# FNet mixing with a gated conv FFN on one core: batch 0's feature row D/2 made by a small FFT at the start, and ScalarE in five weight narrowings

## The chip, the cores and the metric

The kernel runs on one core of one Trainium2 chip. The metric is the device time of one execution in microseconds (us). Before the change three executions took 1222.69, 1222.80 and 1223.03 us, median 1222.8. The profiled execution, from which all durations below come, has a span of 1222.2 us at a granted TensorE clock of 0.999.

## The reference

`x` has 8 batches of 3136 rows (sequence) and 256 columns (features), in fp32. The weights come in as 64-bit floats.

```python
X = np.fft.fft(np.fft.fft(x, axis=1), axis=2).real      # FNet mixing
h = np.maximum(X @ w_in, 0.0)                           # 256 -> 1024
conv_out[:, s] = sum_k conv_w[k] * h[:, s + k - 1]      # 3 taps, zero padded
out = (h * sigmoid(conv_out)) @ w_out                   # 1024 -> 256
```

## The kernel before, in words

**The mixing.** The sequence transform is cut by symmetry. `load_ops` (line 111) loads a batch in two halves: plain rows by SP, mirrored rows by POOL's indirect DMAs. `fold_ops` (line 143) adds and subtracts them on VectorE (DVE) into eight operands `w`. `units` (line 272) multiplies these by cosine and sine tables on TensorE (PE) and makes `PQ`, the transforms P and Q for half the frequencies. The other half follows by symmetry in each step. Half of the tables are loaded, the others are made from them by ScalarE (ACT) in `mirror_tables` (line 235), and `mend_row` (line 229) halves one row.

**The feature D/2.** One of the 129 independent feature columns, number 128, does not fit beside the others. For batches 1 to 7 class `Feature` (line 374) makes it by an FFT of 56 x 56: `gather` (line 417) reads 3136 single elements of `x` into `y`; `tables` (line 421) makes small twiddle tables on ACT; `stage` 0 and 2 (line 441) are small matmuls, 1 a multiplication on DVE, 3 a copy and a store to the DRAM row `ed`. `spread` (line 463) broadcasts the row to 128 partitions, `eb`. For batch 0 the row is made along the main path: `feature()` (line 327) with 16 one-column matmuls, its copies (line 345) and additions on POOL (lines 353 and 354), `row` and `flip` (lines 360 and 364), a store (line 369) and `spread`.

**The weights.** `narrow` (line 508) turns 64-bit floats into fp32 by seven DVE operations, lines 515 to 522: exponent bits out, bias changed, exponent shifted into place, sign put in, mantissa in two operations, product. `w_in` has four parts, `w_out` is narrowed in four of two chunks each. `blocks(i)` (line 587) multiplies the feature transform into part i of `w_in` and gives `G`; `column(i)` (line 604) does so for the feature D/2 and gives `ge`.

**The steps.** Work runs in 256 steps (batch, chunk of four, feature block of eight). In step s: `seed` (line 633) writes `eb * ge` into the PSUM tile `pa` on ACT; `products` (line 653) adds P in `pa` and puts Q in `pb`; in the first 20 steps, named triple, a third product adds Q to `pa` too. `copies` (line 664) moves to SBUF on ACT, `combine` (line 677) on DVE ends the row `h`, `first_tap` (ACT) and `other_taps` (DVE, line 694) are the convolution, `sigmoid` (ACT) and `gate` (DVE and POOL) follow, `mm2` (line 723) is the last product on PE. In the first four steps (`FIRST`) there is no seed: a 1-row product of `er` and `left` stands in its place (line 660), and steps 4 and 5 have a product by zeros (line 640).

**The order.** The schedule is by hand: each engine gets its instructions in the order of the code, and runs them in that order. The main loop is

```python
sigmoid(t-2); products(t+1); copies(t+1); run("act"); combine(t); run("dve")
seed(t+2); first_tap(t); other_taps(t-1); gate(t-2); run("load"); mm2(t-3); run("pe")
```

and a table `side` puts further work into a step: the narrowing of the last part of `w_in` into step 0, of `w_out` into steps 2, 3, 5 and 7, the folds of batch 1 into steps 9 to 19, `Feature` from step 5. Ahead of the loop come the loads, fold and units of batch 0. Two memsets of one element (lines 119 and 575) hold SP's second load and its table loads until POOL has issued its indirect loads. `keep_on` (line 748) issues 16 filler matmuls, in the order of PE ahead of the first unit. DMAs take one of eight semaphore lanes in turn, and a DMA waits until the one before on its lane has landed.

Of the kernel before, what the change touches and what calls it, by code (L numbers as in the profile page):

```python
# [30 lines left out]
FIRST = 4  # L31
# [7 lines left out]
def kernel(  # L39
# [33 lines left out]
    ep = ctx.enter_context(tc.tile_pool(name="ep", bufs=2))  # L73
    erp = ctx.enter_context(tc.tile_pool(name="erp", bufs=1))
# [28 lines left out]
    xh, wt, ea = {}, {}, {}  # L103
# [3 lines left out]
    sg = const.tile([P, 2, 2], F32, name="sg")  # L107
    nc.gpsimd.memset(sg[:, 0], -1.0)
    nc.gpsimd.memset(sg[:, 1], 1.0)
# [33 lines left out]
    def fold_ops(b):  # L143
# [3 lines left out]

        def half(h):
# [27 lines left out]
            def feats(odd):  # L176
                def f():
                    if h == 0 and odd:
                        wt[b] = [wp.tile([P, 4, HQ, P], F32, name="w", tag="w%d" % i) for i in range(2)]
                        if b == 0:  # L180
                            ea[b] = ep.tile([P, 2, HQ], F32, name="ea", tag="ea")
                            nc.gpsimd.memset(wt[b][0][0:KR, 2:4, :, P - 1:P], 0.0)
                    w, s = wt[b][odd], 6 * odd
                    v = t()[k, s:s + 2]
                    lo, hi = v[:, :, :, 1:P], v[:, :, :, D - 1:P:-1]
                    vt(w[k, 0:2, qs, 1:P], lo, hi, op=ALU.add)  # L186
                    vt(w[k, 2:4, qs, 0:P - 1], lo, hi, op=ALU.subtract)  # L187
                    nc.gpsimd.tensor_copy(w[k, 0:2, qs, 0], v[:, :, :, 0])
                    if b:
                        nc.gpsimd.memset(wt[b][odd][k, 2:4, qs, P - 1:P], 0.0)  # L190
                    elif odd:
                        gt(w[k, 2:4, qs, P - 1], t()[k, 7:5:-1, :, P], sg[k], op=ALU.mult)
                    else:
                        nc.gpsimd.tensor_copy(ea[b][k, :, qs], v[:, :, :, P])
                return f
# [9 lines left out]
    PQ, eb, er = {}, {}, {}  # L205
# [36 lines left out]
    class Unit:  # L242

        def __init__(self, b, mms, copy, fin, own=False):
            self.own, self.b, self.mms, self.copy_, self.fin_ = own, b, mms, copy, fin

        def matmuls(self, i, n):
            if i == 0:
                self.p = spare() if self.b == 0 and not self.own else psd.tile([P, 512], F32, name="pd", tag="pd")
            c = [len(self.mms) * j // n for j in (i, i + 1)]  # L250
            for f in self.mms[c[0]:c[1]]:
                f(self.p)
# [19 lines left out]
    def units(b):  # L272
# [54 lines left out]
        def feature():  # L327

            mms = []
            for i in range(2):  # L330
                for j, qs in enumerate(((3, 1), (2, 0))):
                    for c in range(2):
                        n = HO // 2 + 1 - c
                        o = 32 * (2 * j + c)
                        mms.append(product((slice(o, o + 1), slice(0, n)),
                                           lambda k, q, c=c: ea[b][0:k, c, q:q + 1], 0, qs[i],
                                           slice(c, HE, 2), i == 0, i == 1))

            def copy(p):
                a_["e"] = [asp.tile([P, HO + 2], F32, name="as", tag="as") for _ in range(2)]  # L340
                for j in range(2):
                    for c in range(2):
                        n = HO // 2 + 1 - c
                        o = 32 * (2 * j + c)
                        nc.scalar.copy(out=a_["e"][c][0:1, j * n:(j + 1) * n], in_=p[o:o + 1, 0:n])

            def fin(p):
                t = er[b]
                nh = HO // 2
                for c in range(2):  # L350
                    n = nh + 1 - c
                    a, bb = a_["e"][c][0:1, 0:n], a_["e"][c][0:1, n:2 * n]
                    gt(t[:, 2 * c:Q4 + 1:4], a, bb, op=ALU.add)
                    gt(t[:, M - 2 * c:Q4:-4], a[:, 0:nh], bb[:, 0:nh], op=ALU.subtract)
            return Unit(b, mms, copy, fin, True)

# [3 lines left out]
        def row():  # L360
            er[b] = erp.tile([1, NK], F32, name="er", tag="er")
            nc.sync.dma_start(out=er[b], in_=PQ[b][1][P - 1:P, :])

        def flip():

            act(er[b][:, 3:NK:4], er[b][:, 3:NK:4], AF.Copy, scale=-1.0)

        def store():
            nc.sync.dma_start(out=ed[b:b + 1, 0:NK], in_=er[b])

        return (begin, [odd_even(1), odd(1), even(1, 0), even(1, 1), feature(), odd_even(0), odd(0),
                        even(0, 0), even(0, 1)], row, flip, store)

    class Feature:

# [4 lines left out]
        def place(self):  # L380
            H, t = self.H, erp.tile([P, NK], F32, name="ft", tag="er")
# [24 lines left out]
            n = (RC + NQ - 1) // NQ  # L406
            self.l = [f[:, 0:2 * HE].rearrange("p (s i) -> p s i", s=2),
                      f[:, 2 * HE:2 * HE + 2 * H].rearrange("p (s i) -> p s i", s=2)]
            for r, v in enumerate(self.l):
                for s in range(2):  # L410
                    nc.gpsimd.memset(v[0:1, s], 1.0 - s)
                    w = v.shape[2]
                    nc.scalar.dma_start(out=v[1:1 + n * NQ, s], in_=bass.AP(
                        tensor=dft_seq.tensor, offset=dft_seq.offset + (2 * r + s) * NQ * HE,
                        ap=[[4 * NQ * HE, n], [HE, NQ], [1, w]]))

        def gather(self, b, b0):
            nc.sync.dma_start(out=self.y[self.K, b - b0].unsqueeze(2), in_=bass.AP(
# [44 lines left out]
    def spread(b, cs):  # L463

        for c in cs:
            ch = chunks[c]
            eb[b, c] = ebp.tile([P, HN], F32, name="eb", tag="eb")[:, 0:ch.k1 - ch.k0]
            nc.sync.dma_start(out=eb[b, c], in_=ed[b:b + 1, ch.k0:ch.k1].to_broadcast([P, ch.k1 - ch.k0]))
# [39 lines left out]
    def narrow(dst, raw):  # L508
# [7 lines left out]
        ts(out=d, in0=d, scalar1=-896, scalar2=0, op0=ALU.add, op1=ALU.max)  # L516
        ts(out=d, in0=d, scalar1=23, scalar2=None, op0=lsl)
        stt(out=d, in0=hi, scalar=-0x80000000, in1=d, op0=ALU.bitwise_and, op1=ALU.bitwise_or)

        ts(out=hi, in0=hi, scalar1=0xFFFFF, scalar2=0x100000, op0=ALU.bitwise_and, op1=ALU.bitwise_or)  # L520
        stt(out=lof, in0=lo.bitcast(U32), scalar=2.0 ** -32, in1=hi, op0=ALU.mult, op1=ALU.add)
        stt(out=dst, in0=lof, scalar=2.0 ** -20, in1=dst, op0=ALU.mult, op1=ALU.mult)

    class Weight:
# [14 lines left out]
        def narrow(self, c0, c1):  # L539
            if self.raw is not None:  # L540
                narrow(self.dst[:, c0:c1], self.raw[:, c0:c1])
# [19 lines left out]
    def raw_in(i):  # L561
        def f(sh):
# [6 lines left out]
            for i in range(4)]  # L569
    w_cv.load(nc.scalar)  # L570
    for h in range(2):
# [15 lines left out]
    def blocks(i):  # L587


# [6 lines left out]
        if 2 * i < FIRST:  # L596
            p = spare()
            for t in range(2):
                mm(p[0:1, N4:2 * N4], dm[:, t, 1, P - 1:P], w[:, t], t == 0, t == 1)
            nc.scalar.copy(out=left[0:1, 2 * i:2 * i + 2].rearrange("p f i -> p (f i)"), in_=p[0:1, N4:2 * N4])  # L600
# [3 lines left out]
    def column(i):  # L604
        w, p = w4[i], spare()
# [14 lines left out]
    def start_all(p, l, r):  # L620

        mm(p, l, r, True, True)

# [4 lines left out]

    def first(s):

        return s[0:2] == (0, 0) and s[2] < FIRST

    def seed(s):
# [4 lines left out]
        if not first(s):  # L638
            if s in ((0, 0, FIRST), (0, 0, FIRST + 1)):
                start_all(pa[s].rearrange("p (t n) -> p t n", t=2), dm[:, 0, 0], w4[0])  # L640
            act(pa[s][:, 0:n], eb[b, c], AF.Copy, scale=ge[:, f:f + 1])  # L641
# [11 lines left out]
    def products(s):  # L653
# [4 lines left out]
        mm(pa[s][:, 0:n], G[:, 0, fs], PQ[b][0][:, ch.k0:ch.k1], first(s), not triple(s))  # L658
        if first(s):
            mm(pa[s][:, 0:n], left[0:1, f, :], er[b][:, ch.k0:ch.k1], False, False)  # L660
# [87 lines left out]
    def keep_on(n):  # L748

        for _ in range(n):  # L750
            mm(idle[:, 0:2 * P], wt[0][1][0:NP, 1, 0], wt[0][1][0:NP, 0, 0:2], True, True)

    begin, us, row, flip, store = units(0)
    begin()

    nc.gpsimd.memset(PQ[0][1][96:P, :], 0.0)
    for f in fold_ops(0):
        f()

    odds = [us[j] for j in (0, 1, 5, 6)]  # L760
    w_in[0].narrow(0, 2)
    keep_on(16)
# [3 lines left out]
    for i in range(4):  # L766
        for j, u in enumerate(odds):
            u.part(i)
            if i == 3:
                u.copy()  # L770
                u.fin()
                if j == 1:
                    row()
# [5 lines left out]
    for i, u in enumerate(us[j] for j in (2, 4, 3, 7, 8)):  # L779
# [3 lines left out]
    flip()  # L783
    store()
    spread(0, range(len(chunks)))
    for f in load_ops(1, 0, nc.sync):
        f()
    blocks(0)
# [10 lines left out]
    at(0, "dve", lambda: w_in[3].narrow(0, 2))  # L799
    for i in (0, 1):  # L800
        at(i, "pe", lambda i=i: column(i))
    for cycle, c in ((2, 0), (3, 2), (5, 4), (7, 6)):
        at(cycle, "dve", lambda c=c: w_out.narrow(c, c + 2))
# [14 lines left out]
    feat = Feature()  # L818
    at(5, "load", feat.place)
    for c, b0, b1 in ((6, 1, min(4, B)), (21, 4, B)):  # L820
        for b in range(b0, b1):
            at(c + b - b0, "load", lambda b=b, b0=b0: feat.gather(b, b0))
    for i in range(3):
        at(11 + i, "act", lambda i=i: feat.tables(i))
# [5 lines left out]
    for b in range(1, B):  # L830
        begin, us, *_ = units(b)
        us = us[0:4] + us[5:]
# [31 lines left out]
    copies(steps[0])  # L864
    for t in range(n + LAG):
# [90 lines left out]
```

## Time and profile before

| what | from the profile of before |
|---|---|
| span; median of three runs | 1222.2 us; 1222.8 us |
| PE busy | 1187.9 us (97%), 4876 matmuls |
| DVE busy | 1126.0 us (92%) |
| ACT, POOL busy | 877.0 us (72%), 370.9 us (30%) |
| DVE busy from 64 to 74, 74 to 84, 84 to 94, 94 to 104 us | 9.76, 9.72, 9.72, 9.93 of 10 |
| PE busy in the same stretches | 10.00, 10.00, 8.91, 9.63 |
| start of `mm2` of steps 0 and 5 on PE | 69.89 and 94.37 us |
| one seven-operation narrowing on DVE, step 2 | 58.36 to 62.26 us |
| gather of one feature column, issue on SP | 0.86 to 2.30 us |

A group of instructions in the profile is named by line, engine, operation and "output<-inputs"; matmuls are all issued by the helper in line 94, so the tile tells them apart (`pd<-tab,ea` is the feature row of batch 0, `pb<-w` before the first unit is the filler). An fp32 matmul appears as two records. What stands in brackets after a row is the idle time before it and what ended it. Idle time on an engine that is not on the chain of work costs nothing.

### The profile page before, as it was taken

What the parts mean: (1) busy time and instruction counts of PE and PEld (TensorE: products, weight loads), DVE (VectorE), ACT (ScalarE), POOL (GpSimd) and SP (SyncE); (2) the same over time, 40 slices, a digit from 0 to 9 for tenths busy, and PEclk for the clock granted to TensorE, in tenths of its full rate; (3) what the DMA queues carried; (4) which work ended last, traced back from release to release, by engine and by line L of the source; (5) the groups of instructions that cost most, each with busy time, mean ns of one, the idle gap of its engine ahead of it and who ended that gap; (6) DMA issues with size and microseconds to landing.
All of it is one profiled execution on the core that took longest, in us unless ns stands there. A gap on an engine that the chain in (4) does not pass through costs nothing.

```text
span 1222.2 us, 15450 instructions
## 1 busy us (share of the span) xinstructions
PE 1187.9 (97%) x4876; PEld 907.5 (74%) x4876; DVE 1126.0 (92%) x1696; ACT 877.0 (72%) x1832; POOL 370.9 (30%) x474
## 2 busy tenths in 40 slices
PE   5999999999999999999999999999999999999998
PEld 4676777667777777677777777777777787777776
DVE  7799978998999999999999999999998888899996
ACT  2467666777677777777777777777777777788884
POOL 5224532244142413242324242232222122222222
PEclk9999999999999999999999999999999999999999
DMA  9512242112031210211111020310001000110000
GB/s 235 180 8 79 81 48 60 54 54 72 6 99 42 75 50 32 76 55 53 53 57 59 22 79 27 86 47 26 27 1 53 31 26 27 46 33 27 26 27 31
DMA packets 70213, 66.30 MB, mean 54 GB/s; under 512 B 28123, under 2 KB 57827, under 8 KB 70131
## 3 DMA queue, kind: packets, MB, share of 16 engines
q1 hardware_dynamic: 64493, 52.18, 15.0%
q0 software_dynamic: 5120, 12.85, 3.4%
q8 instruction: 39, 0.64, 0.2%
q14 instruction: 43, 0.35, 0.1%
q10 hardware_dynamic: 518, 0.28, 0.1%
HBM read 39.53 MB, written 25.74 MB: 53 GB/s over the span
## 4 chain that ended last, share of the span: by engine, by line
PE 68%; DVE 22%; issue 4%; ACT 2%; DMA 0%; DVEq 0%; SPq 0%; ACTq 0%
PE po L94 42%; PE pb L94 10%; PE pa L94 10%; DVE g L698 7%; PE pd L94 7%; DVE h L686 4%; DVE g L719 3%; DVE xh L158 2%; DVE xh L169 1%; ACT nb L675 1%; DVE w L186 1%; DVE w L187 1%; DVE xh L173 0%; ACT g L711 0%; DVE pt L291 0%
## 5 line engine op out<-in xcount | busy, mean ns | idle before, releaser
L94 PE MATMUL po<-wout,g 128*128 128x256 f32 x3072 | 709.9, 381 | 13.8 <-DVE g L719 13.3
L94 PEld LDWEIGHTS po<-wout,g 128*128 128x128 f32 x3072 | 579.0, 190 | 168.8 <-DVE g L719 50.7
L698 DVE SCALAR_TENSOR_TENSOR g<-h,cw,g 128x770 f32<-128x770 f32 (+1 forms) x512 | 548.9, 1072 | 9.3 <-ACT g L692 0.2
L718 POOL TENSOR_TENSOR g<-g,h 128x385 f32<-128x385 f32 (+1 forms) x256 | 232.5, 909 | 781.3 <-ACT g L711 523.1
L711 ACT ACTIVATE g<-g 128x385 f32<-128x385 f32 (+2 forms) x512 | 244.4, 527 | 196.8 <-DVE g L698 196.2
L675 ACT ACTIVATE nb<-pb 128x386 f32<-128x386 f32 (+2 forms) x472 | 208.1, 494 | 85.9 <-PE pb L94 85.2
L686 DVE CUSTOM_DVE_ANT_0 h<-pa,nb 128x386 f32<-128x386 f32 (+2 forms) x492 | 255.6, 559 | 3.7 <-ACT h L672 3.7
L692 ACT ACTIVATE g<-h,cw 128x770 f32<-128x770 f32 (+1 forms) x256 | 243.4, 951 | 0.2 <-DVE h L686 0.2
L94 PE MATMUL pb<-qt,G 127*128 127x387 f32 (+2 forms) x512 | 212.8, 496 | 0.0
L94 PE MATMUL pa<-pt,G 128*128 128x387 f32 (+2 forms) x512 | 211.9, 495 | 0.0
L641 ACT ACTIVATE pa<-eb,ge 128x387 f32<-128x387 f32 (+2 forms) x252 | 151.7, 602 | 1.3 <-PE pa L94 0.7
L94 PEld LDWEIGHTS pa<-pt,G 128*128 128x128 f32 x512 | 96.9, 189 | 73.5 <-issue 17.9
L719 DVE TENSOR_TENSOR g<-g,h 128x385 f32<-128x385 f32 (+1 forms) x256 | 146.2, 571 | 0.9 <-ACT g L711 0.9
L94 PE MATMUL pd<-tab,w 98*128 98x196 f32 (+3 forms) x448 | 122.5, 374 | 0.0
L133 POOL DMA_INDIRECT xh<-in_x_dram,idx x64 | 106.5, 1665 | 13.4 <-issue 9.6
L94 PEld LDWEIGHTS pb<-qt,G 127*128 127x128 f32 x512 | 94.6, 190 | 17.4 <-issue 0.9
L94 PEld LDWEIGHTS pd<-tab,w 98*128 98x128 f32 (+1 forms) x448 | 84.0, 191 | 12.5
L738 ACT COPY os<-po 128x256 f32<-128x256 f32 x196 | 57.6, 394 | 8.4 <-PE po L94 4.6
L158 DVE TENSOR_TENSOR xh<-xh 98x1020 f32<-98x1020 f32 (+1 forms) x32 | 40.8, 1283 | 2.4 <-DMA xh<-in_x_dram,idx 2.4
L169 DVE TENSOR_TENSOR xh<-xh 98x1024 f32<-98x1024 f32 (+1 forms) x32 | 42.1, 1314 | 0.1
L291 DVE TENSOR_TENSOR qt<-as,pd 128x197 f32<-128x197 f32 (+1 forms) x14 | 7.2, 516 | 21.7 <-ACT as L287 21.7
L291 DVE TENSOR_TENSOR pt<-as,pd 128x197 f32<-128x197 f32 (+1 forms) x14 | 7.3, 520 | 20.2 <-ACT as L287 20.2
(114 smaller groups left out, 405.6 us busy)
## 6 DMA issues: line engine op xcount, KB each, us to landing
out_dram<-os SPq DMA_DIRECT2D x192, 128.0 KB
xh<-in_x_dram SPq DMA_DIRECT2D x16, 784.0 KB
eb<-ed SPq DMA_DIRECT2D x16, 193.5 KB
tab<-dft_seq_dram SPq DMA_DIRECT2D x4, 589.5 KB
raw<-in_moe_w_in_dram SPq DMA_DIRECT2D x4, 512.0 KB
raw<-in_moe_w_out_dram SPq DMA_DIRECT2D x1, 2048.0 KB
eb<-ed SPq DMA_DIRECT2D x8, 209.0 KB
eb<-ed SPq DMA_DIRECT2D x8, 193.0 KB
```

Source lines behind the costliest of these rows:

```text
L94: nc.tensor.matmul(o, l, r, start=start, stop=stop, skip_group_check=True)
L133: nc.gpsimd.indirect_dma_start(out=xh[b, h][0:NP, 7 - m].rearrange("p q d -> p (q d)"), out_offset=None, in_=bass.AP(tensor=x.tensor, offs ...
L158: vt(a[:, :, :, 1:D], a[:, :, :, 1:D], r[:, :, :, D - 1:0:-1], op=ALU.add)
L641: act(pa[s][:, 0:n], eb[b, c], AF.Copy, scale=ge[:, f:f + 1])
L675: act(nb[s][:, i, cols], p[:, cols], AF.Copy, scale=-1.0 if i else 1.0)
L686: nc.vector._custom_dve(TENSOR_ADD_SAT, out=to, in0=a[:, cols], in1=c[:, i, cols], s0=BIG, s1=0.0)
L692: act(gs[s], hs[s][:, 0:n], AF.Copy, scale=cw[:, 0, s[2]:s[2] + 1])
L698: stt(out=g, in0=h[:, k:k + n], scalar=cw[:, k, f:f + 1], in1=g, op0=ALU.mult, op1=ALU.add)
L711: act(gs[s][:, c], gs[s][:, c], AF.Sigmoid)
L718: gt(g[:, p], g[:, p], h[:, p], op=ALU.mult)
L719: vt(g[:, v], g[:, v], h[:, v], op=ALU.mult)
L738: nc.scalar.copy(out=osb[:, j % 2], in_=pt[:, j % 2])
```

## The change

- Batch 0 uses `Feature` too. Its place, gather, table loads, `tables` and stages move to the very start; gather and loads are issued by ACT between the conv weight and the zero rows. Stages 0 to 3 stand among the fold operations of half 0, after the sixth of seven.
- `feature()`, `row`, `flip`, `store`, the `ea`, `er` and `sg` tiles, the 1-row products and the products by zeros go. All steps are seeded. Chunk 0 of the row is broadcast by POOL behind the fold, chunks 1 to 3 by SP.
- The filler is 8 matmuls of 512 columns (six into one bank, one each into two others) for 16 of 256.
- `column(0)` stands ahead of `blocks(0)`, `column(1)` behind the products of step 0; they were in steps 0 and 1.
- In five narrowings (the last part of `w_in`, all of `w_out`) ACT computes the exponent: one activation for two DVE operations. The mantissa goes to a spare tile, and the sign is put in after it.

```diff
-        ts(out=d, in0=d, scalar1=-896, scalar2=0, op0=ALU.add, op1=ALU.max)
-        ts(out=d, in0=d, scalar1=23, scalar2=None, op0=lsl)
-        stt(out=d, in0=hi, scalar=-0x80000000, in1=d, op0=ALU.bitwise_and, op1=ALU.bitwise_or)
-        ts(out=hi, in0=hi, scalar1=0xFFFFF, scalar2=0x100000, op0=ALU.bitwise_and, op1=ALU.bitwise_or)
-        stt(out=lof, in0=lo.bitcast(U32), scalar=2.0 ** -32, in1=hi, op0=ALU.mult, op1=ALU.add)
+        if room is not None:
+            act(d, d, AF.Relu, scale=2.0 ** 23, bias=low[0:d.shape[0]])
+        else:
+            ts(out=d, in0=d, scalar1=-896, scalar2=0, op0=ALU.add, op1=ALU.max)
+            ts(out=d, in0=d, scalar1=23, scalar2=None, op0=lsl)
+            stt(out=d, in0=hi, scalar=-0x80000000, in1=d, op0=ALU.bitwise_and, op1=ALU.bitwise_or)
...
+        ts(out=sg, in0=hi, scalar1=0xFFFFF, scalar2=0x100000, op0=ALU.bitwise_and, op1=ALU.bitwise_or)
+        stt(out=lof, in0=lo.bitcast(U32), scalar=2.0 ** -32, in1=sg, op0=ALU.mult, op1=ALU.add)
+        if room is not None:
+            stt(out=d, in0=hi, scalar=-0x80000000, in1=d, op0=ALU.bitwise_and, op1=ALU.bitwise_or)
...
+    feat = Feature()
     w_cv.load(nc.scalar)
+    feat.place()
+    feat.gather(0, 0, nc.scalar)
+    feat.load()
...
-        if not first(s):
-            if s in ((0, 0, FIRST), (0, 0, FIRST + 1)):
-                start_all(pa[s].rearrange("p (t n) -> p t n", t=2), dm[:, 0, 0], w4[0])
-            act(pa[s][:, 0:n], eb[b, c], AF.Copy, scale=ge[:, f:f + 1])
+        act(pa[s][:, 0:n], eb[b, c], AF.Copy, scale=ge[:, f:f + 1])
...
-        mm(pa[s][:, 0:n], G[:, 0, fs], PQ[b][0][:, ch.k0:ch.k1], first(s), not triple(s))
-        if first(s):
-            mm(pa[s][:, 0:n], left[0:1, f, :], er[b][:, ch.k0:ch.k1], False, False)
+        mm(pa[s][:, 0:n], G[:, 0, fs], PQ[b][0][:, ch.k0:ch.k1], False, not triple(s))
...
-    nc.gpsimd.memset(PQ[0][1][96:P, :], 0.0)
-    for f in fold_ops(0):
+    ops = fold_ops(0)
+    for f in ops[0:6]:
         f()
+    for i in range(4):
+        feat.stage(i, 0, 1)
+    for f in ops[6:]:
+        f()
+    spread(0, [0], nc.gpsimd)
...
-    at(0, "dve", lambda: w_in[3].narrow(0, 2))
-    for i in (0, 1):
-        at(i, "pe", lambda i=i: column(i))
+    at(0, "dve", lambda: w_in[3].narrow(0, 2, room))
     for cycle, c in ((2, 0), (3, 2), (5, 4), (7, 6)):
-        at(cycle, "dve", lambda c=c: w_out.narrow(c, c + 2))
+        at(cycle, "dve", lambda c=c: w_out.narrow(c, c + 2, room))
```

## The prediction

> **What bounds the kernel now.** I read the page first (busy shares, chain), then the timeline of the first 110 us, then the chain of waits of that stretch.
>
> ```profile
> PE 1187.9 (97%) x4876; PEld 907.5 (74%) x4876; DVE 1126.0 (92%) x1696; ACT 877.0 (72%) x1832; POOL 370.9 (30%) x474
> ...
> PE 68%; DVE 22%; issue 4%; ACT 2%; DMA 0%; DVEq 0%; SPq 0%; ACTq 0%
> ```
>
> PE is full over the whole, but the change touches the first 100 us, and there the bound changes hands three times. The head, from the timeline (start, us, engine, line):
>
> ```profile
> 2.01 1.19 POOL L133 DMA_INDIRECT xh<-in_x_dram,idx  x1 [0.26 <-issue]
> ...
> 8.38 2.35 DVE L158 TENSOR_TENSOR xh<-xh 98x1020 f32<-98x1020 f32 x2 [2.40 <-DMA xh<-in_x_dram,idx]
> ...
> 15.18 0.68 DVE L174 TENSOR_TENSOR xh<-xh 98x512 f32<-98x512 f32 x1
> ...
> 15.36 10.57 PE L94 MATMUL pb<-w 98*128 98x256 f32 x32 [8.66 <-POOL w L188]
> ...
> 25.77 8.10 PE L94 MATMUL po<-tab,w 98*128 98x196 f32 x32
> ```
>
> POOL's indirect loads release the fold at 8.38; the fold runs on DVE without a hole; filler matmuls hold PE from 15.36; the first useful product starts where they end, 25.77. The next hand-over is in the chain (start, us, what):
>
> ```profile
> 54.93 2.35 PE pa L94 x6
> ...
> 57.36 0.50 ACT h L672
> ...
> 57.89 0.56 DVE h L686
> ```
>
> PE carries the chain from 34.77 to 57.3, DVE from 57.9: seven-operation narrowings, taps and gates, then folds, to 149.15, where PE takes over to the end. So the end moves by what the DVE chain has moved at about 95 us.
>
> [...] 256-column filler matmuls start 0.427 us apart from 15.36 to 22.2, then 0.216 apart, so 6.85 us are slow. [...] in the trace every ACT instruction starts in program order. [...] the DMA share is 0.63 in the first 8 us and 0.90 to 1.02 from 8 to 34, so little room is left.
>
> **Part 1: up to the first useful product.**
> - POOL, ahead of its first indirect load: two iotas 0.37 (old L400), a wait for DVE's 0.16 us AND with two hand-overs of 0.1, a tensor_scalar 0.19 (L403), four memsets 0.90 (L411). Two small memsets go, one comes: about -0.03. Sum +1.8. All eight loads, the 1-element memset that releases SP's second load, and the one that releases SP's tables stand behind it.
> - DMA: three gathers keep the share up from 64.8 to 71.0; the windows sum to 5.26 us of all engines, 1.75 each. The four table reads (80 to 84) take 0.76. These 2.5 us fit into the idle 37% of the first 8 us and the hole that POOL leaves. I take +0.1; bounds 0 and +0.7 (all of the 2.5 instead of POOL's 1.8).
> - ACT issues: gather (0.86 to 2.3 each on SP) and four reads at 0.81 stand ahead of the zero rows and table load, then about 3 us of small ft activations. ACT is idle from 6.9 to 22.9: hidden.
> - DVE: two 56x112 products behind L167. The 56x336 form takes 0.488; estimate 0.25 each, 0.45 for both. Everything behind on DVE moves too.
> - PE: the filler now stands behind eight stage-2 matmuls, 0.143 apart warm (136.8 to 137.9): 1.2 with hand-over 0.1 more. So filler starts at 15.87 + 1.9 + 0.45 + 0.1 + 1.2 + 0.1 = 19.6 instead of 15.36.
> - The filler has the same 4096 columns, 16 matmuls of 512 at 0.853 slow or 0.432 fast. Slow for 6.85 us from its own start: 8 + 8, end 29.9. Slow time counted from the stage-2 matmuls at 18.3: end 29.3. [...] I take 29.5.
>
> **+3.7** (bounds +2.5 and +4.9). The mirrored tables allow it: ACT makes them from 22.95 to 28.06 and the last is needed at about 31.8. But the new store of the feature row on ACT waits, in the built program, for the semaphore lane of the third big table read. Packets put that landing near 26; with +2 it is 28, the mirrors then end at 33.1, the last is needed at 35.5: 2.4 us spare. The row's broadcast on POOL then lands by about 38, needed at 48.
>
> **Part 2: PE from 34.8 to DVE's combine at 57.89** (times as in before, without the +3.7). Removed on PE: feature products 0.88, 1-row products 0.96 per block twice, er products 0.84 in each of four steps, two zero products 0.86 each. Removed elsewhere: L345 1.31, L366 0.93, two L600 0.36 on ACT; POOL's L353/354; SP's row copy and store. Moved: column(0) and column(1), 0.97 each, ahead of blocks(0) and step 1. Added: four seeds of 0.59 on ACT. Blocks(0) waits anyway for DVE's eight additions (40.3 to 43.3), which gain only 0.4, so the first 1.8 us of PE's savings are lost: step 0 starts at 44.4 (was 44.27). Without er: h(0) at 46.8 (47.62). Step 1 follows column(1): h(1) at 49.7 (50.60). Step 2: h(2) at 55.4 (57.36); combine(2) at 55.95, **-1.9**.
>
> **Part 3: the narrowings.** Each drops L516 and L517, 0.46 apart by starts: -0.92 on DVE. ScalarE's replacement on 128x512 is 0.70 (from L641, 0.584 at 386, and L692, 0.928 at 770[...]). It is emitted after the next step's copies, so it queues behind them, and DVE's OR and last product wait for it. In step 0 the wait is 1.4 us, which eats the gain (combine(1) 52.2, was 52.52). In step 2 it is worst:
>
> ```profile
> 60.89 1.28 ACT L711 ACT_TABLE_LOAD   x1
> 62.18 0.94 ACT L711 ACTIVATE g<-g 128x385 f32<-128x385 f32 x2
> 63.02 0.47 ACT L670 ACTIVATE nb<-pb 128x385 f32<-128x385 f32 x1
> 63.86 0.49 ACT L672 ACTIVATE h<-pa 128x385 f32<-128x385 f32 x1 [0.37 <-PE pa L94]
> ```
>
> All four stand ahead. With ACT 2.6 us earlier there, the exponents are ready at 61.95; DVE has done its three operations at 58.0: a 3.9 us wait, behind which stand the last product, the taps, the gate and thereby mm2(1). combine(3) comes at 65.8 (was 65.22): +0.55. From then on ACT is one DVE step behind (the sigmoid waits for the taps), so sigmoid, copies and exponents (2.6 us) fit beside combine and three operations: steps 3, 5, 7 gain 0.92 each, -2.7. At combine(8): 0.55 - 2.7 = **-2.15** (bounds -0.6, if ACT is late each time, and -5.6: the 1.9 plus four times 0.92, no wait at all). PE's demand from mm2(0) on, 4.55 us a step, stays below it.
>
> **Part 4, at nothing:** the ft tables leave steps 11 to 13 (ACT, 3 us, beside a full DVE); feature stages of other batches stay; SP's spread of three chunks is 10 us early.
>
> **Sum:** +3.7 - 2.15 = +1.55 on a span of 1222.2, so 1223.8. The median of the runs, 1222.8, is 0.6 above that span: 1224.3.
>
> **Rivals.**
> 1. Near even, as summed: 1224.3, own range 1222.3 to 1226.3. Chance 0.53.
> 2. Slower: DMA and lanes decide. The gather and its reads delay the first half by 2.5 instead of 1.9, the store holds the mirrors until they, not the filler, release the odd products (another 1.2), and ACT is late in steps 3, 5, 7 (-1.0 in place of -2.15): +5.5 - 1.0 = +4.5, 1227.3. It decides once the third table read lands after 30.4, when the spare 2.4 us are gone. For it: DMA share 1.0 and 3 to 7 us to landing; against: the early hole. Chance 0.25.
> 3. Faster: ScalarE is reached early. PE's removed matmuls let the copies finish before DVE asks, steps 0 and 2 wait little (-5.0)[...]: -2.5 and less, 1220.0. For it: the PE savings are real; against: table load and sigmoid stand in order. Chance 0.14.
> 4. The change doesn't do what it says: the row is not early, since store and POOL broadcast wait for lanes; the seeds then come after 48 and PE waits: +3 to +4, 1226. Against: 10 us of spare. Chance 0.08.
>
> **Numbers.** 0.2% of 1222.8 is 2.4 us, about what a measurement of this kernel can tell. Of the first case, a quarter lies above 1225.2. So slower 0.13 + 0.22 + 0.06, same 0.40 + 0.04, faster the rest, rounded: 0.15, 0.45, 0.40. The range leaves one in ten out on either side, ends reaching into rivals 2 and 3: 1220.8 to 1227.4.
>
> **What would show it.** Right: first POOL indirect at 3.8; first fold operation near 10.3; filler from 19.6; first odd product near 29.5; a DVE wait of about 4 us for the exponents in step 2 and none above 0.7 in steps 3, 5, 7; mm2 at step 8 later by 1.5. Wrong: odd products released by ACT's mirrors or by DMA (rival 2), no DVE wait in step 2 (rival 3), seeds ended by the broadcast (rival 4). The forecast fails if filler warm-up or the queue ahead of the exponents differs by more than 2 us.

## The result, and the profile after

| | median, us | lowest to highest, us | against the kernel before, 95% interval |
|---|---|---|---|
| before | 1222.78 | 1222.69 to 1223.03 | |
| after | 1230.03 | 1227.70 to 1230.61 | 1.0055 (1.0038 to 1.0073) |

The change made the kernel slower by 7.2 us. The prediction was 1224.3 us with a range to 1227.4: its sum, +1.55 us, was far too small. The profiled execution has a span of 1228.7 us, 6.5 above that of before.

I take the views in the order of the prediction. `mm2(16)`, where PE takes over to the end, starts at 155.85 us (149.15 before), and from there to the end both kernels take the same (1072.9 and 1073.0 us). So all of the loss lies ahead of it. The 6.7 us split at the end of the odd products (start of the 32nd record `po<-tab,w`) and at `combine(8)` on DVE:

| | before | after | moved by | predicted |
|---|---|---|---|---|
| last odd product | 33.38 | 43.03 | +9.65 | +3.7 |
| from there to `combine(8)` | 60.85 | 57.85 | -3.00 | -2.15 |
| from there to `mm2(16)` | 54.92 | 54.97 | +0.05 | 0 |

The two rows of `combine(8)`, from the timelines of before and of after:

```profile
94.23 0.55 DVE L686 CUSTOM_DVE_ANT_0 h<-pa,nb 128x386 f32<-128x386 f32 x1
```

```profile
100.88 0.55 DVE L631 CUSTOM_DVE_ANT_0 h<-pa,nb 128x386 f32<-128x386 f32 x1
```

The second part of the sum did what was said, and a little more. The first was off by 6 us. The timeline of after shows it (start, us, engine, line; in brackets the idle time before the row and what ended it):

```profile
2.48 7.00 ACTq L360 DMA_DIRECT2D ft<-dft_seq_dram  x4
...
3.43 1.20 POOL L127 DMA_INDIRECT xh<-in_x_dram,idx  x1 [0.21 <-issue]
...
11.12 1.22 DVE L151 TENSOR_TENSOR xh<-xh 98x1020 f32<-98x1020 f32 x1 [4.57 <-DMA xh<-in_x_dram,idx]
...
14.59 1.22 DVE L151 TENSOR_TENSOR xh<-xh 98x1020 f32<-98x1020 f32 x1 [2.25 <-DMA xh<-in_x_dram,idx]
...
20.25 0.68 DVE L167 TENSOR_TENSOR xh<-xh 98x512 f32<-98x512 f32 x1
...
22.23 7.64 PE L91 MATMUL pb<-w 98*128 98x512 f32 x12
...
31.42 2.14 PE L91 MATMUL po<-tab,w 98*128 98x196 f32 x8
...
33.66 1.90 ACT L224 ACTIVATE tab<-tab 99x392 f32<-99x392 f32 x4 [11.12 <-DMA ed<-ft]
...
35.61 7.91 PE L91 MATMUL po<-tab,w 98*128 98x196 f32 x24 [2.05 <-ACT tab L224]
```

There are two breaks to see. POOL starts its indirect loads 1.42 us later than before (3.43 for 2.01), but the fold 2.74 later, and its second operation stands another 2.25 us for DMA, where before it followed at once; the last step of half 0 comes at 20.25 for 15.18. The second break is on ACT: the mirrored tables start at 33.66 for 22.95, released by `ed<-ft`, the store of the feature row that stands ahead of them. In before their own tables released them:

```profile
22.95 1.97 ACT L239 ACTIVATE tab<-tab 99x392 f32<-99x392 f32 x4 [16.03 <-DMA tab<-dft_seq_dram]
```

PE begins the odd products at 31.42, stops for 2.05 us until the mirrors come, and then takes 7.91 us for 24 records.

The windows view of before and of after for 4 to 8 us (stretch, us, busy time of PE, weight load, DVE, ACT, POOL, then granted clock, DMA share, GB/s) tells what the first break is:

```profile
4.00:6.00 2.00, 0.00 (x0) 0.00 (x0) 1.77 (x7) 0.95 (x1) 1.44 (x2) 1.00 1.02 297
6.00:8.00 2.00, 0.59 (x2) 0.50 (x2) 0.00 (x0) 0.18 (x1) 1.73 (x3) 1.00 0.71 203
```

```profile
4.00:6.00 2.00, 0.00 (x0) 0.00 (x0) 1.52 (x6) 0.00 (x0) 1.60 (x2) 1.00 1.02 203
6.00:8.00 2.00, 0.58 (x2) 0.49 (x2) 0.52 (x2) 0.00 (x0) 1.49 (x2) 1.00 1.44 79
```

The DMA engines are full and move little: 79 GB/s at a share of 1.44 (the view counts a packet's whole time where the packet starts, so a share can pass 1). Nearly all of the gather's 3136 packets of 4 bytes, some 3040, run from 4.9 to 7.9 us. The chain of waits tells what the second break is (start, us, what):

```profile
22.23 10.93 DMA tab<-dft_seq_dram
...
33.23 0.44 DMA ed<-ft
33.68 1.89 ACT tab L224 x4
...
35.61 7.91 PE po L91 x24
```

The store waits in ACT's queue for the lane of the third big table read, issued at 22.23 (16.21 before) and landed at 33.16: in the trace ACT waits from the end of the row's copy, 22.5, to 33.18 for semaphore 100, which both DMAs use. And the windows of after from 34 us show why 24 records took 7.91 us:

```profile
34.00:36.00 2.00, 0.39 (x2) 0.39 (x3) 1.07 (x2) 1.98 (x5) 0.00 (x0) 1.00 1.05 285
36.00:38.00 2.00, 2.00 (x8) 1.41 (x7) 0.00 (x0) 1.97 (x5) 0.00 (x0) 0.74 0.87 257
38.00:40.00 2.00, 2.00 (x5) 1.37 (x5) 0.00 (x0) 0.63 (x2) 0.00 (x0) 0.50 1.02 389
40.00:42.00 2.00, 2.00 (x8) 1.29 (x8) 0.00 (x0) 0.10 (x1) 0.45 (x1) 0.90 1.05 399
```

After the stop PE's granted clock falls to 0.50, by the trace's record of it from 36.97 to 40.38 us. So a stop of 2 us cost nearly 4.

### The profile page after: what moved, and what is told of

It is laid out like the page before. It is cut to its first block, busy times and chain, and to the rows that moved or that the text cites. A ratio compares the mean times of both kernels' runs of the same rounds, so it can differ in the third digit from the quotient of the medians.

```text
span 1228.7 us, 15369 instructions
## 1 busy us (share of the span) xinstructions
PE 1182.5 (96%) x4834; PEld 900.7 (73%) x4834; DVE 1120.6 (91%) x1688; ACT 880.1 (72%) x1835; POOL 364.3 (30%) x468
## 4 chain that ended last, share of the span: by engine, by line
PE 71%; DVE 19%; issue 4%; ACT 2%; DMA 2%; POOL 1%; DVEq 0%; SPq 0%; ACTq 0%; POOLq 0%
PE po L91 44%; PE pb L91 10%; PE pa L91 10%; PE pd L91 7%; DVE g L643 6%; DVE h L631 3%; DVE g L664 3%; DVE xh L151 2%; DVE xh L162 1%; DMA xh<-in_x_dram 1%; DMA tab<-dft_seq_dram 1%; ACT nb L620 1%; DVE w L176 1%; DVE w L177 1%; DVE xh L166 0%
## 5 line engine op out<-in xcount | busy, mean ns | idle before, releaser
L588 ACT ACTIVATE pa<-eb,ge 128x387 f32<-128x387 f32 (+2 forms) x256 | 154.2, 602 | 0.7 <-ACT ft L406 0.6
L178 POOL COPY w<-xh 98x4 f32<-98x4 f32 (+1 forms) x32 | 19.1, 596 | 26.4 <-DVE xh L162 13.2
```

## The experiments

Each ratio is against the kernel before on the same chip. The chips differ: beside the changed kernel the median of before was 1222.8 us, beside the others 1223.3 to 1223.6. "Odd end" is the start of the last odd product.

| run | median, us | ratio to before, 95% | fold, last step of half 0 | filler | first odd | mirrors | odd end | `combine(8)` |
|---|---|---|---|---|---|---|---|---|
| before | | | 15.18 | 15.36 | 25.77 | 22.95 | 33.38 | 94.23 |
| after | 1230.03 | 1.0055 (1.0038 to 1.0073) | 20.25 | 22.23 | 31.42 | 33.66 | 43.03 | 100.88 |
| e1_runs | 1224.79 | 1.0015 (1.0006 to 1.0024) | 16.31 | 18.28 | 28.53 | 29.43 | 37.17 | 95.06 |
| e2_store | 1225.78 | 1.0020 (1.0012 to 1.0028) | 19.20 | 21.18 | 30.30 | 27.47 | 37.91 | 95.75 |
| e5_both | 1223.86 | 1.0003 (0.9995 to 1.0011) | 16.60 | 18.57 | 28.89 | 24.54 | 36.49 | 94.37 |
| e6_gather | 1225.10 | 1.0013 (1.0006 to 1.0020) | 17.82 | 15.60 | 25.20 | 25.76 | 33.48 | 94.56 |
| e10_filler | 1226.54 | 1.0026 (1.0015 to 1.0036) | 19.43 | 17.20 | 27.52 | 28.07 | 35.80 | 96.60 |
| e3_seven | 1227.88 | 1.0040 (1.0025 to 1.0054) | 19.21 | 21.19 | 30.44 | 32.29 | 41.68 | 99.73 |
| e4_split357 | 1226.74 | 1.0025 (1.0014 to 1.0036) | 19.49 | 21.57 | 31.07 | 33.24 | 42.61 | 97.91 |
| e8_narrow | 1222.60 | 0.9995 (0.9987 to 1.0003) | 15.96 | 15.39 | 24.65 | 23.80 | 32.26 | 93.07 |
| e7_best | 1220.84 | 0.9975 (0.9964 to 0.9985) | 15.28 | 14.74 | 24.54 | 23.01 | 32.67 | 91.61 |
| e9_early | 1223.29 | 1.0002 (0.9994 to 1.0011) | 18.55 | 16.32 | 27.22 | 27.60 | 35.86 | 93.30 |
| e11_order | 1224.84 | 1.0009 (1.0000 to 1.0017) | 16.12 | 13.89 | 22.74 | 22.98 | 37.28 | 95.18 |
| e12_between | 1224.36 | 1.0006 (0.9998 to 1.0014) | 16.46 | 14.23 | 24.31 | 23.23 | 37.42 | 91.95 |

A profile is one execution, and heads differ from run to run: the fold's last step of half 0 comes at 20.25, 19.20, 19.21 and 19.49 in four kernels that are the same up to there (after, e2_store, e3_seven, e4_split357). Differences inside a profile are firmer than those between two.

### The gather alone, the store alone, and both

The first pair undoes one suspected cause each in the changed kernel, the third run undoes both.

**e1_runs**, 56 packets of 224 bytes for 3136 of 4:

```diff
-                ap=[[RC * D, RC], [D, RC], [1, 1]]))
+                ap=[[RC * D, RC], [1 if b == 0 else D, RC], [1, 1]]))
```

> The first gather reads 56 runs of 56 neighbouring elements instead of 3136 single ones: the same bytes in 56 packets, so batch 0's feature row D/2 is computed from other data. Theory A (the 3136 packets hold all DMA engines from 5 to 8 us, and the backlog lets the second half's load in among the last loads of the first): the second fold operation, at 14.59 after the change, comes by 11.5 to 12.5, the fold stands 2 to 3 us earlier, and the time falls by 2 to 4 us, to about 1226 to 1228. Rival B (POOL's set-up and the four table reads make the delay): the second fold operation stays within 0.7 us of 14.59, the time within 1 us of 1230.

1224.79 us: most of the loss is gone. In its windows the gap of 4 to 8 us has closed:

```profile
4.00:6.00 2.00, 0.03 (x1) 0.06 (x1) 1.62 (x7) 0.00 (x0) 1.60 (x2) 1.00 0.87 266
6.00:8.00 2.00, 0.56 (x2) 0.44 (x2) 0.00 (x0) 0.52 (x1) 1.49 (x2) 1.00 0.72 219
```

The fold's last step comes at 16.31, 1.13 us later than before. POOL's later start, 1.42 us, is enough to explain that; no run undoes it alone. The store still holds the mirrors until 29.43, but the third table read now lands at 28.9, and PE's stop is short:

```profile
28.53 2.14 PE L91 MATMUL po<-tab,w 98*128 98x196 f32 x8
...
31.44 6.22 PE L91 MATMUL po<-tab,w 98*128 98x196 f32 x24 [0.77 <-ACT tab L224]
```

After 0.77 us of idleness the 24 records take 6.22 us, not 7.91: PE kept its clock.

**e2_store**, the gather as it is, the row's copy, store and first broadcast behind the second group of mirrors:

```diff
-    for i in range(4):
+    for i in range(3):
         feat.stage(i, 0, 1)
...
-    spread(0, [0], nc.gpsimd)
...
     mirror_tables(2)
+    feat.stage(3, 0, 1)
+    spread(0, [0], nc.gpsimd)
```

> The copy and store of batch 0's feature row, with their wait for a DMA lane, stand behind the mirrored tables on ACT instead of ahead of them; nothing else moves. Theory A (the lane wait holds the mirrors, PE stops for 2 us and falls back to half rate for 3.4 us): mirrors start near 26 to 27 instead of 33.66, PE has no stop between the filler and the end of the odd products, no slow spacing of 0.65 us there, time -4 (3 to 5), about 1226. Rival B (the odd products wait for something else too, such as the table reads themselves): under 1.5 us.

1225.78 us. The fold is late as in the changed kernel (19.20), but the mirrors start at 27.47, and PE does not stop:

```profile
27.47 1.94 ACT L224 ACTIVATE tab<-tab 99x392 f32<-99x392 f32 x4 [11.20 <-DMA tab<-dft_seq_dram]
...
30.30 8.10 PE L91 MATMUL po<-tab,w 98*128 98x196 f32 x32
```

**e5_both**, both edits:

> Batch 0's gather reads 56 contiguous runs (so batch 0's row D/2 is computed from other data), and the stage-3 copy, store and first broadcast stand behind mirror_tables(2) on ACT. My theory (two separate causes at the head, the gather's 4-byte packets and the store ahead of the mirrors): both go, the first odd product stays near 28.2 us as with the runs alone, the odd products run without a stop (7.6 us), and the time is about 1 us below that of the runs alone, near 1223.7 us, level with the kernel before. Rival (the two are one cause, the late table reads): the time stays at that of the runs alone, 1224.8 us.

1223.86 us, not told apart from before, as the theory had it. The four runs make a square. The odd products end at 43.03 with both causes, 37.17 without the gather's packets, 37.91 without the store in front, 36.49 without either. So the gather costs 1.4 us at that point when the store is out of the way and 5.9 when it is not; the store costs 0.7 us without the small packets and 5.1 with them. The loss is not a sum: 4.4 of 6.5 us come only when both are there, since the packets delay the table reads and the store hands that delay to the mirrors, and the stop, 2.05 us, then costs PE its clock (0.77 us did not). The size of this joint part is less sure than its cause. Two other profiles with both causes, e3_seven and e4_split357, end the odd products at 41.68 and 42.61, which makes it 3.1 or 4.0 us, and the four ratios of the table give 2.8 us, with an uncertainty about as large. What is left with neither, +3.1 us at the odd end, is the prediction's Part 1, which had 3.7 with almost nothing for DMA. (At the odd end the packets cost less than the 2.6 us at the fold, since the filler in e2_store happened to be 1.2 us shorter than in e5_both.)

### The gather by itself

**e6_gather**, the kernel before with one DMA more:

```diff
     w_cv.load(nc.scalar)
+    spot = const.tile([P, RC], F32, name="spot")
+    nc.scalar.dma_start(out=spot[0:RC].unsqueeze(2), in_=bass.AP(
+        tensor=x.tensor, offset=x.offset + P, ap=[[RC * D, RC], [D, RC], [1, 1]]))
```

> The kernel before with one thing added: the 56x56 gather of 4-byte elements as the second DMA on ACT's queue, into a tile that nobody reads. My theory: its 3136 packets alone hold up the first loads, so the fold's last step of half 0 (15.18 us before) comes 2 to 4 us later, and the time is 2 to 4 us longer. The prediction's step: 0 to 0.7 us, hidden in the idle third of the first 8 us. Rival: the gather does harm only together with POOL's later start (the held load of half 1 falls among half 0's indirect loads); then it is below 1 us here too.

The fold's last step is 2.64 us later (17.82), so the packets do it alone, without POOL's later start or the table reads. But the kernel is only 1.5 us slower (0.4 in the profiled execution). In this profile the filler was also 0.8 us shorter than in before. The timeline tells where the rest went:

```profile
15.60 8.97 PE L94 MATMUL pb<-w 98*128 98x256 f32 x32 [8.46 <-POOL w L188]
...
25.20 2.22 PE L94 MATMUL po<-tab,w 98*128 98x196 f32 x8 [0.64 <-DMA tab<-dft_seq_dram]
...
27.74 6.22 PE L94 MATMUL po<-tab,w 98*128 98x196 f32 x24 [0.32 <-ACT tab L239]
```

In the kernel before, the filler waits for POOL, not for the fold, and starts 0.24 us later only; the mirrors are 2.8 us later (25.76) and had nearly that much to spare. The changed kernel has put the filler behind fold, stage 1 and stage 2, and spends the slack.

**e10_filler**, the changed kernel with the filler straight behind half 0's fold and the row's stages behind it (0 behind the filler, 1 behind the fold, 2 and 3 behind the odd products):

```diff
-    for f in ops[0:6]:
-        f()
-    for i in range(4):
-        feat.stage(i, 0, 1)
-    for f in ops[6:]:
+    for f in ops:
         f()
-    spread(0, [0], nc.gpsimd)
...
+    feat.stage(0, 0, 1)
+    feat.stage(1, 0, 1)
     mirror_tables(0)
...
+    feat.stage(2, 0, 1)
+    feat.stage(3, 0, 1)
+    spread(0, [0], nc.gpsimd)
     mend_row(0, half)
```

> The changed kernel with its gather, POOL set-up, ACT queue and narrowings as they are; only the places of the row's stages move: the filler straight behind half 0's fold, stage 0 behind the filler, stage 1 on DVE behind the whole fold, stages 2 and 3, store and broadcast behind the odd products. My theory: the gather's delay of the fold reaches PE only because the filler stands behind fold, stage 1 and stage 2; freed of them the filler starts near 18 us, the first odd product comes near 28, and with the store out of the mirrors' way the time is near 1223.5, 6 us below the changed kernel's and 1 to 2 us below that with the store alone moved. Rival: the mirrors, behind the late table reads, hold the odd products all the same; then it equals the run with the store moved, 1225.8, or more.

The first half of the theory held: filler at 17.20, first odd product 27.52, odd end 35.80, 2.1 us earlier than with the store alone moved. The time did not follow: 1226.54, no better than e2_store. The even products start at 38.57 after 1.78 us of idleness (0.96 in e2_store), PE's clock falls to 0.50 again, the even products take 7.44 us for 5.85, and the seeds of step 0 wait 0.89 us for the row. A later row gave back what an earlier filler had won.

### The narrowings

**e3_seven** and **e4_split357**: no narrowing split in the changed kernel, and only those of steps 3, 5 and 7.

```diff
-    at(0, "dve", lambda: w_in[3].narrow(0, 2, room))
+    at(0, "dve", lambda: w_in[3].narrow(0, 2))
...
-        at(cycle, "dve", lambda c=c: w_out.narrow(c, c + 2, room))
+        at(cycle, "dve", lambda c=c: w_out.narrow(c, c + 2))
```

In e4_split357 the last line is

```diff
+        at(cycle, "dve", lambda c=c: w_out.narrow(c, c + 2, room if c else None))
```

> All narrowings with seven DVE operations as before the change, the rest of the change kept. Theory A (the split about breaks even: it loses 1.5 and 3.8 us of waits in steps 0 and 2 and gains 0.92 five times): within 1.5 us of the changed kernel, 1229 to 1231, the wait of 3.8 us in step 2 gone and seven operations in its place. Rival B (the waits for ScalarE are a main cause of the loss): 3 us or more faster, 1227 or less.

> ScalarE forms the exponents in steps 3, 5 and 7 alone; steps 0 and 2 have seven DVE operations. Theory A (the waits of steps 0 and 2 eat what the split saves there, and the three later splits save 0.92 each): 1.5 to 3 us faster than the kernel with seven operations everywhere, 1 to 2.5 faster than the changed kernel. Rival B (PE, not DVE, is the bound in steps 3 to 8, so that the split saves nothing): equal to the kernel with seven operations within 0.7 us.

The heads of these runs differ, so the part behind the odd products is the measure. From their end to `combine(8)` it is 57.85 us with all five split, 58.05 with none, 55.30 with three. Splitting all five is worth 0.2 us, splitting three 2.75. From one combine to the next, e4_split357 is faster than e3_seven by 1.18, 0.82 and 0.85 us in steps 3, 5 and 7, 2.85 in all, of which 0.1 goes ahead of `combine(3)`. The splits of steps 0 and 2 do more than lose their own saving: they cost 2.6 us, nearly all that the three others gain. The timeline of after shows why:

```profile
60.50 0.69 DVE L480 SCALAR_TENSOR_TENSOR win<-raw,win 128x512 int32<-128x512 int32 x1 [1.50 <-ACT win L468]
...
70.97 0.69 DVE L480 SCALAR_TENSOR_TENSOR wout<-raw,wout 128x512 int32<-128x512 int32 x1 [3.78 <-ACT wout L468]
...
77.15 0.69 DVE L480 SCALAR_TENSOR_TENSOR wout<-raw,wout 128x512 int32<-128x512 int32 x1
```

DVE's OR waits 1.50 us for the exponents in step 0 and 3.78 in step 2, and not at all in step 3. With none split, odd end to `combine(8)` is 2.8 us shorter than before: that is the gain of PE's removed products, the prediction's Part 2.

**e8_narrow**, the kernel before with the new `narrow`, split in steps 3, 5 and 7:

```diff
-        at(cycle, "dve", lambda c=c: w_out.narrow(c, c + 2))
+        at(cycle, "dve", lambda c=c: w_out.narrow(c, c + 2, room if c else None))
```

> The kernel before with ScalarE's exponents in steps 3, 5 and 7 and nothing else. My theory: 0.92 us a step off the DVE chain, -2.75 us in all, 1220.8 us. Rival: the gain needs the shorter queue on ACT that the removed products make; then DVE waits for the exponents and it is below 1 us.

The rival held. The head of this run is 1.1 us ahead of the one of before, and from `combine(2)` to `combine(8)` it takes 36.30 us, as before (36.34). Steps 5 and 7 gain 0.82 and 0.85 us, step 3 loses 1.62, because there ACT is late:

```profile
69.31 0.70 DVE L532 SCALAR_TENSOR_TENSOR wout<-raw,wout 128x512 int32<-128x512 int32 x1 [3.24 <-ACT wout L520]
```

The median, 1.0 us lower, has an interval that takes in no change. So a split pays only where ACT is ahead of DVE, and in step 3 that needs the rest of the change: from `combine(2)` to `combine(8)` e4_split357 takes 33.58 us.

### A version that beats both

**e7_best** keeps the removed products and the splits of steps 3, 5 and 7, and takes the row out of the head. `place` is cut up, so that its POOL work stands behind the indirect loads and its DVE operation behind the fold:

```diff
-    feat.gather(0, 0, nc.scalar)
-    feat.load()
...
     load_tables(1)
+    feat.iotas()
     w_in[0].load(nc.sync)
+    feat.load(nc.sync)
+    feat.gather(0, 0, nc.sync)
     load_tables(0)
...
     mirror_tables(2)
+    for i in range(3):
+        feat.tables(i)
     for i in range(4):
+        if i == 3:
+            feat.stage(0, 0, 1)
+            feat.stage(1, 0, 1)
...
+    feat.stage(2, 0, 1)
+    feat.stage(3, 0, 1, nc.gpsimd)
+    spread(0, [0], nc.gpsimd)
     mend_row(0, half)
```

> The changed kernel with the feature row late: its table reads and gather on SP behind w_in[0]'s load, POOL's set-up behind the eight indirect loads, the filler straight behind the fold, the ft activations behind mirror_tables(2), stages 0 and 1 ahead of the odds' last round, stage 2 behind the odds, store and broadcast from POOL, and ScalarE's exponents only in steps 3, 5 and 7. My theory: head as before (first odd product 25.8, odd products end at 34), the 2.8 us of PE's removed products and 2.75 us of narrowings are kept, so mm2(16) comes 4.5 to 5.5 us earlier and the time is near 1218.5. Rival: the row comes too late (the seeds of step 0 wait for the broadcast past 45 us) or the even tables do, and the gain shrinks to 2 us or less, 1221.5 or more.

1220.84 us, 0.25% below before (0.15 to 0.36%) and some 9 us below the changed kernel. It is the only kernel of the study whose interval lies wholly below 1, and 2.3 us short of what was hoped. The gather costs here too. Windows, then timeline:

```profile
22.00:24.00 2.00, 2.00 (x6) 0.92 (x5) 1.97 (x4) 0.99 (x3) 0.00 (x0) 1.00 0.66 149
24.00:26.00 2.00, 2.00 (x9) 1.37 (x8) 1.97 (x6) 1.98 (x5) 0.69 (x2) 1.00 1.05 25
```

```profile
36.65 7.43 PE L91 MATMUL po<-tab,w 99*128 99x197 f32 x32 [2.98 <-ACT tab L218]
```

For 2 us the engines move 25 GB/s at a share of 1.05. The two big reads of the even tables, next in SP's queue, are issued only by 27.2, and the even products start after 2.98 us of idleness and take 7.43 us for the 5.85 of e5_both.

So the second branch of the rival, late even tables, took part of the gain.

Three attempts to mend that by the order of the queues did not; the edits are against e7_best. In **e9_early** the gather is ACT's second DMA again, the table reads stand behind the zero rows, and the small activations on `ft` ahead of the mirrors (that part is not shown):

```diff
     feat.place()
+    feat.gather(0, 0, nc.scalar)
...
+    feat.load(nc.scalar)
     load_tables(1)
     w_in[0].load(nc.sync)
-    feat.load(nc.sync)
-    feat.gather(0, 0, nc.sync)
```

> As the run with the late row, but the gather is ACT's second DMA again and the four table reads stand on ACT behind the zero rows, so that SP's order is that of the kernel before; the ft activations stand ahead of the mirrors. Row D/2 is still made behind the filler (stage 0 and 1 ahead of the odds' last round). My theory: the fold is late by the gather's 2 to 3 us but filler and mirrors have that much to spare, as in the gather run; the 3 us wait for tables(0) in front of the even products goes; mm2(16) near 144.5 us, time near 1218.5. Rival: with the gather early the third table read and the mirrors come late enough to hold the odd products by 2 us or more, and the time is that of the late row or worse, 1221 or more.

The time is the rival's, but not for its reason: PE waits only 0.17 us for the mirrors. The fold is 3.4 us later than before, the odd products end at 35.86, PE then stands 1.49 us, its clock drops (0.50 in the window of 40 to 42 us), and nothing is gained over before. That stop ends 0.09 us after ACT's `mend_row(0)`, which stands behind the copy of the row. In **e11_order** the even tables stand ahead of the row's reads, `mend_row(0)` ahead of stage 2, and w_out's load behind the broadcasts:

```diff
+    load_tables(0)
     feat.load(nc.sync)
     feat.gather(0, 0, nc.sync)
-    load_tables(0)
...
+    mend_row(0, half)
     feat.stage(2, 0, 1)
...
-    mend_row(0, half)
...
     spread(0, range(1, len(chunks)))
+    w_out.load(nc.sync)
```

> As the run with the late row, with SP's order mended: tables(0) stand right behind w_in[0]'s load as in the kernel before, the row's table reads and gather behind them, w_out's load behind the broadcasts; ACT does mend_row(0) ahead of the stage-3 copy. My theory: the late row lost 3 us only because SP stood with tables(0) behind the gather's lane, and the even products waited for them; with that gone the even products follow the odd ones at about 34.5 us, combine(2) comes at 55 to 55.5 (57.9 before), mm2(16) near 144 and the time is near 1218.3. Rival: the gather then holds w_in[1] or the row itself is late for step 0's seeds (44.7 us), and the time stays at the late row's 1220.8 us.

In **e12_between**, which is that kernel with one more exchange, the row's reads stand ahead of the even tables and the gather behind:

```diff
+    feat.load(nc.sync)
     load_tables(0)
-    feat.load(nc.sync)
     feat.gather(0, 0, nc.sync)
```

> As the run with SP's order mended, but the row's table reads stand ahead of tables(0) and the gather behind them: w_in[0], table reads, tables(0), gather, dm, w_in[1..3], broadcasts, w_out. My theory: what follows the gather on its queue waits some 2.5 to 4.5 us for it; with only dm and w_in[1..3] behind it, the table reads land by 25 us, tables(0) by 29, PE has no stop of over 2 us between odd and even products and keeps its clock; combine(2) comes near 55.5 us and the time is near 1218.5. Rival: stage 0 waits for the gather past 31 us or the even products for w_in[1]'s narrowing, PE stops for over 2 us, falls to half rate, and the time is 1221 or more.

In both the rival held in its kind (in e12_between in the median of 1224.4; its profiled run was one of the quickest): stage 0 stands in PE's order ahead of the last round of odd products, and waits for the row's inputs. In e12_between:

```profile
26.45 5.99 SPq L547 DMA_DIRECT2D dm<-dft_dim_dram  x1
...
33.78 0.37 PE L91 MATMUL pd<-ft 56*56 56x112 f32 x2 [3.36 <-DMA ft<-in_x_dram]
...
34.08 3.93 PE L91 MATMUL po<-tab,w 99*128 99x196 f32 x8
```

The gather was issued at 25.53 and held PE until 33.78; the load behind it on SP, whose issue takes 0.62 us in the kernel before, took 5.99; and eight odd records took 3.93 us after the stop for 2.25 in e7_best. In e11_order PE stood 4.11 us for the row's tables, with the DMA engines at 18 GB/s:

```profile
30.00:32.00 2.00, 0.00 (x0) 0.00 (x0) 0.78 (x2) 0.80 (x5) 0.00 (x0) 0.85 0.65 18
32.00:34.00 2.00, 0.68 (x3) 0.40 (x3) 0.00 (x0) 1.94 (x17) 0.00 (x0) 0.50 0.61 168
...
42.00:44.00 2.00, 2.00 (x7) 2.00 (x7) 1.90 (x4) 0.33 (x1) 1.39 (x3) 0.50 0.69 144
```

Here the clock, by the windows, stayed at 0.50 from 31.4 us to beyond 44, though PE was busy again from 33.32. It did not come back as soon as in the changed kernel (3.41 us), and no run shows why. e12_between tells how much that matters: the profiled execution, with 3.4 us at 0.50, took 1221.5 us at a mean granted clock of 0.998; those of 1224.6 us and more have 0.994 to 0.996.

Whether the row's stages could stand clear of both the odd and the even products was not tried.

## Why the prediction was wrong

- **The step that failed** is in Part 1: "These 2.5 us fit into the idle 37% of the first 8 us and the hole that POOL leaves. I take +0.1; bounds 0 and +0.7". Measured at the fold it is 2.6 us (e6_gather against before, e2_store against e5_both) to 3.9 (after against e1_runs). I asked only whether there was room in the sum over 8 us. But 1.7 of the 3.0 us of idle engine time lay in the first 2 us (share 0.14 in before), and from 4 to 6 us the share was 1.02 already. The packets begin some 3.5 us after their issue (1.44, 4.9) and run all at once, when the fold's first loads are on their way. The windows show that the other loads got little then: 79 GB/s in all from 6 to 8 us, for 203 in before.
- **The term that hung on it** is "2.4 us spare" before the mirrors, from a third table read that lands at 28. It landed at 33.16, and the last mirrors ended at 38.6, 3.1 us after the time for which the prediction needed them. The prediction named this wait, in rival 2, but set the point from which it decides (30.4) too late: it asked when PE needs the last mirrors, and PE stops for the first ones, after 8 of the 32 records, 2.1 us from the first odd product. In e1_runs a landing at 28.9 stopped PE already, for 0.77 us. The prediction gave the wait 1.2 us; with the gather's packets there the store costs 5.1 at the odd end. The rest is PE's clock: the prediction costed a stop as its length, and left out the slow time after it (0.50 from 36.97 to 40.38 us).
- **Other terms of Part 1.** POOL's set-up put the first indirect load 1.42 us back (taken 1.8); without the small packets the fold's last step is 1.13 to 1.42 us late (e1_runs, e5_both). From the end of the fold's step to the filler it is 1.30 us (taken 1.85). The filler ran 9.2 us (taken 9.9); the lower bound of +2.5 was an estimate with a shorter slow time than before shows (6.85 us). With both causes removed the odd products are +3.1 late, near the +3.7 of the sum. These terms were right in kind; that they came so near is in part luck, since the length of the filler differs by 1.5 us between profiles.
- **Part 2** was right in kind: -1.9 was taken at `combine(2)`. Seen from the odd end it is -2.3 with the first split and -2.9 without.
- **Part 3** was right in its steps: waits of 1.50 and 3.78 us (taken 1.4 and 3.9), activation 0.71 (taken 0.70), no wait above 0.7 in steps 3, 5 and 7. The gains there are 1.18, 0.82 and 0.85 us, 2.85 in all (taken 0.92 each, 2.7 in all).
- **Part 4** held for what it names: the first seeds did not wait for the broadcast in the changed kernel. The small activations on ACT, which Part 1 called hidden, were: they end at 19.4 us, ahead of the fold's last step.
- **The rivals.** Rival 2 is what happened, outside its size and without its last term: ACT was not late in steps 3, 5 and 7. Rival 3 failed at its first condition, waits in steps 0 and 2. Rival 4 failed: the row was in time.

## What to carry to other kernels

A DMA of many tiny elements is costed by the time for which it fills all engines (here 3 us, 4.9 to 7.9, for 12.2 KB) and by who has loads in flight in that time, not by its bytes or its share of a wide window: try it alone in the unchanged kernel first (2.64 us at the fold here). A DMA on a compute engine's queue can hold that engine's next work for as long as the older transfer on its semaphore lane takes (10.6 us here, from the end of the row's copy to the store), so work that PE waits for goes ahead of it. Before moving an engine's work behind a chain, look whether the old order was absorbing delays of that chain, and look at the granted clock behind a stop of PE, whose cost can be its length plus slow time: in these traces stops up to 1.39 us kept the clock and those of 1.49 to 4.11 us lost it.

## What the runs showed that was not expected

- The gather, 12.2 KB, held back the other traffic wherever it stood: 79 GB/s in a window of 2 us at the head, 25 at 24 us, 18 at 30 us (there at a share of 0.65, so that the engines had room; the `w_in` loads behind the gather on SP were issued only from 31.99). And what followed it on its queue was held: four table reads took 7.00 us to issue behind it on ACT (3.39 in e5_both), one load 5.99 on SP (0.62 in the kernel before).
- PE's clock fell after short stops. With 0.77 and 0.96 us of idleness it stayed (e1_runs, e2_store), and with 1.39 us too (after, 61.00 to 62.39). With 2.05 us it fell to 0.50, and it took until 40.38 us, 4.8 from the restart, to come back. In e9_early it fell to 0.50 with 1.49 us, behind 0.58 us of very small matmuls.
- The slow time did not grow with the stop. The clock was at 0.50 for 3.41 us in after (36.97 to 40.38, stop of 2.05 us) and, by the windows, for 3.4 us in e9_early, e10_filler, e7_best and e12_between, with stops of 1.49, 1.78, 2.98 and 3.36 us; in e11_order, with 4.11 us, it was for more than 12. Nor did the fall keep one distance from the beginning of the stop: 3.4 us in after, 2.2 in e11_order, 3.9 in e7_best. What sets these times no run shows. And the clock is not the same in all executions of a kernel: of e5_both's 13 six have a mean granted clock of 1.000 and take 1222.3 to 1223.2 us, four have 0.998 and take 1225.1 to 1225.7.
- The filler's length was not fixed: 10.4 us from its start to the first odd product before, 9.2 in after, 8.9 in e11_order, with the same columns and with no relation to its start. A slow part at its start goes with it: the spacing of its records halves at 22.3 us in before (0.427 to 0.216), 6.9 us after the filler's start, and at 26.7 in after (0.853 to 0.429), 4.5 us after it; in e11_order the windows hold 3 records from 16 to 18 us and 6 from 18 to 20, so about 4 us are slow. Half of these slow times is 3.5, 2.2 and about 2 us, which leaves, as an estimate, about 6.9 us for the filler at full clock in each. Some 1.5 us of any difference between two heads can come from this alone.
